# A gated S4D and spectral mix on one core: inputs of the states first, ScalarE in the parameters, the first rows from SBUF to SBUF, and one set of magnitudes at the start

## The chip, the cores and the metric

The kernel runs on one core of one Trainium2 chip. The metric is the device time of one execution in microseconds (us), and the median of several runs is compared. Engines are called by the names of the profile: PE is TensorE (PEld its weight loads), ACT is ScalarE, DVE is VectorE, POOL is GpSimd, SP is SyncE, which only issues DMAs here. ACT and POOL issue DMAs too; such issues stand in the profile as ACTq, POOLq and SPq.

## The reference

```python
def reference(A_u, A_log_A_real, A_A_imag, A_C_real, A_C_imag, A_log_dt, A_D_skip, B_x, B_w_r, B_w_i, gate_w):
    # A: u (1, 2048, 640), states N = 128 for each of the 640 channels
    dt = jnp.exp(log_dt)
    A = -jnp.exp(log_A_real) + 1j * A_imag
    C = (C_real + 1j * C_imag) * dt[:, None]
    P = jnp.exp((A * dt[:, None])[:, :, None] * pos[None, None, :])      # 640 x 128 x 2048
    K = 2.0 * jnp.einsum("dn,dnl->dl", C, P).real                        # the response, 640 x 2048
    y = irfft(rfft(u_t, 4096) * rfft(K, 4096))[:, :, :2048]              # long convolution
    a = y.transpose + u * D_skip
    # B: spectral filter of the same u
    b = irfft2(rfft2(u) * (w_r + 1j * w_i))
    g = sigmoid((u * gate_w).sum(-1))
    return g * a + (1 - g) * b
```

All data are f32.

## The kernel before, in words

The Fourier transforms of length 4096 are done as products with tables in two steps. Step 1 (`stage1`, line 335) takes four rows of four channels at a time, which are 16 matmuls in the profile; step 2 (`stage2`, line 348) goes by an index `pr` from 0 to 16, two at a time, each of which is 8 matmuls in the profile. The channels are four chunks `c` of 160, each in two halves `h` of 20 rows.

The program is made of five parts:

- **phase_p**, the parameters. The four inputs of the states (`cr`, `ci`, `ai`, `lar`, 128 x 5 x 128 each) and log_dt (`ld`) are loaded on SP. DVE computes the phase `ph` of C (with an Arctan on ACT) and the logarithm of its magnitude `q` (with an Ln on ACT); POOL computes the angle `th` and the decay `lar` of a step. `parts` splits each result into two f32r summands (a rounding copy, a subtraction) and writes them with a POOL DMA to `par_d` in device memory, where they are read again in another order.
- **phase_a, first half**: the transform of u, chunk by chunk: step 1 from `u`, with ACT evacuating PSUM into `t1` (line 382); the gate's logits (`p_g`, line 417) with weights `z` that POOL prepares (line 394); step 2 with `w2`, evacuated into `ut` and written to `u_d`. `copy` puts the evacuations on ACT until the marker `T.pin` is set and on DVE from then on. `T.pin` is the last matmul of step 2 for chunk 1 and the two indices from `pr` = 8.
- **phase_a, second half**: the spectral filter, nine fronts of 128 rows (lines 473 to 573).
- **phase_b**, the responses: 40 sets `t`, in batches of five (`BT`). `load` reads the `par` tile of a batch from `par_d`. `mags(t)` makes the magnitudes `e`: three matmuls (line 638) and three Exp (line 640). `phases(t)` makes the phases `q` (lines 649 to 652), `trig(t)` four Sin (lines 665 to 668), `prods(t)` the products `x` on DVE and `y` on POOL (lines 675 to 680), and `kgen(t)` 64 matmuls (line 693) into `p_k`. After every second set ACT copies `p_k` to `kt` (line 701); after ten sets `kt`, one tile of 40 rows, goes to `k_d` on SP (line 703).
- **phase_c and phase_d**: step 1 of the response's transform, then products with `u_d`, back transforms, gate and output.

Order: the instructions of an engine are issued in one fixed order, which is settled when the program is built: a scheduler goes by the order in which the code names them and by its own estimate of when they are ready. The code names first `ld` of phase_p (to its `yield`), then the loads of u and the first weights `z`, then the rest of phase_p, then phase_a as far as `T.pin`; from there `merge` interleaves phase_a and phase_c (`ga`, weight 194) with phase_b (`gl`, weight 76.8). `mags` puts each of its matmuls behind `T.pin` on PE, and the first Sin of a set behind the last Exp named before it, and an Exp behind the last Sin, so that ACT's function tables change only where a batch changes.

Of the kernel before, what the change touches and what calls it, by code (L numbers as in the profile page):

```python
# [9 lines left out]
F32 = mybir.dt.float32  # L10
F32R = mybir.dt.float32r
# [8 lines left out]
N = 128  # L20
# [163 lines left out]
def body(tc, A, out):  # L184
    nc = tc.nc
    T = Ctx()
    with ExitStack() as top:
# [7 lines left out]
        c1 = cst.tile([128, A["t_c1"].shape[1]], F32, name="c1")  # L195
        for x in (slice(0, 256), slice(256, c1.shape[1])):
            nc.scalar.dma_start(c1[:, x], A["t_c1"][:, x])
        o = 0
# [33 lines left out]
def phase_p(tc, A, T):  # L232
# [3 lines left out]
    with ExitStack() as ctx:  # L236
# [10 lines left out]
        yield 0.0  # L247
        lar, ai, cr, ci = tn("lar"), tn("ai"), tn("cr"), tn("ci")
        for t, nm in ((cr, "cr_l"), (ci, "ci_l"), (ai, "ai_l"), (lar, "la_l")):
            nc.sync.dma_start(t[:, :, :], A[nm])  # L250
# [19 lines left out]
        def parts(v, i, eng):  # L270
            t = p1.tile([128, 2, 5, N], F32R, name="parts%d" % i)
            eng.tensor_copy(t[:, 0], v[:, :, :])
            eng.tensor_tensor(out=t[:, 1], in0=v[:, :, :], in1=t[:, 0].bitcast(F32), op=ALU.subtract)
            G.dma_start(T.par_d[:, :, i:i + 2].rearrange("y x i z n -> (y x) (i z n)"), t.rearrange("p i z n -> p (i z n)").bitcast(F32))
# [3 lines left out]
        for o, i in ((ar, cr), (ab, ci)):  # L278
            V.tensor_scalar(out=o[:, :, :].bitcast(I32), in0=i[:, :, :].bitcast(I32), scalar1=0x7FFFFFFF, scalar2=None, op0=ALU.bitwise_and)
# [8 lines left out]
        V.tensor_scalar(out=ph[:, :, :], in0=ph[:, :, :], scalar1=1.0 / (2 * math.pi), scalar2=None, op0=ALU.mult)  # L288
        V.tensor_scalar(out=y[:, :, :], in0=ph[:, :, :], scalar1=-2.0, scalar2=0.25, op0=ALU.mult, op1=ALU.add)
        V.tensor_tensor(out=y[:, :, :], in0=y[:, :, :], in1=ab[:, :, :], op=ALU.mult)  # L290
        V.tensor_tensor(out=ph[:, :, :], in0=ph[:, :, :], in1=y[:, :, :], op=ALU.add)
        V.tensor_scalar(out=y[:, :, :], in0=ph[:, :, :], scalar1=-2.0, scalar2=0.5, op0=ALU.mult, op1=ALU.add)
        V.scalar_tensor_tensor(out=y[:, :, :], in0=cr[:, :, :], scalar=0.0, in1=y[:, :, :], op0=ALU.is_lt, op1=ALU.mult)
        V.tensor_tensor(out=ph[:, :, :], in0=ph[:, :, :], in1=y[:, :, :], op=ALU.add)
        V.tensor_scalar(out=y[:, :, :], in0=ci[:, :, :], scalar1=0.0, scalar2=-2.0, op0=ALU.is_lt, op1=ALU.mult)
# [57 lines left out]
def phase_a(tc, A, T):  # L353
# [3 lines left out]
    with ExitStack() as ctx:  # L357
# [44 lines left out]
        for c in range(4):  # L402
            t1 = ta[c % 2].tile([128, 16, 160, 2], F32, tag="t1", name="t1")
            t1v = t1.rearrange("p x d y -> p d x y")
            for h in range(2):
# [15 lines left out]
                if c < 3:  # L421
                    zs.append(weights(c + 1, h))
# [554 lines left out]
```

## Time and profile before

| | |
|---|---|
| time, median of 3 runs | 618.22 us (616.89 to 624.77) |
| the profiled execution's own time | 616.28 us |
| its span in the profile | 614.5 us, so 1.8 us lie around it |
| busy share of the span | PE 88%, PEld 67%, DVE 81%, ACT 59%, POOL 43% |
| DMA | 101.98 MB, mean 166 GB/s |

Busy shares are means over stages with different limits. The span has three stretches: the start, up to the first matmul of a response at 54.19 us; the middle, where `ga` and `gl` run beside each other, up to the first step 2 of phase_d at 437.84 us; and phase_d up to the end. The change touches the first and, through the order of the streams, the middle. The views that show waits name the engine and line that a wait ended on.

### The profile page before, as it was taken

To read this page: it belongs to the slowest core of one execution; us is meant where nothing else is said; L and a number is where in the kernel's file an instruction comes from. 1 tells how busy PE (TensorE), PEld (TensorE's weight loads), DVE (VectorE), ACT (ScalarE), POOL (GpSimd) and SP (SyncE) were. 2 spreads that over 40 slices of the span, in tenths; PEclk is the share of its full clock that TensorE was granted. 3 is DMA by queue.
4 is the path that set the end of the run, shared out by engine and by line. 5 is a ranking of instruction groups with operands and counts; after the bars stand their busy time and mean duration, and the time that the engine had idled before them with its cause. 6 is when DMAs were issued, how large, how long until landed. Compare 5 with 4: busy or idle time off the path is not lost.

```text
span 614.5 us, 16646 instructions
## 1 busy us (share of the span) xinstructions
PE 539.0 (88%) x7084; PEld 411.1 (67%) x7084; DVE 500.0 (81%) x748; ACT 364.6 (59%) x659; POOL 267.2 (43%) x246
## 2 busy tenths in 40 slices
PE   9688989989968989989799989898989979998864
PEld 6576667766746666766667766566878768787731
DVE  6961697598899988999999999978496975987863
ACT  4556675677847777897599897798523213231210
POOL 4921261152527344455326334345243546565450
PEclk9899989989979987999799999999989989999987
DMA  8787204154512411243242122115967989799985
GB/s 340 304 290 248 70 25 167 30 200 153 215 44 65 138 44 54 66 137 109 65 139 69 36 87 89 49 45 183 349 228 264 259 264 325 230 298 288 260 217 195
DMA packets 47987, 101.98 MB, mean 166 GB/s; under 512 B 3220, under 2 KB 32680, under 8 KB 46152
## 3 DMA queue, kind: packets, MB, share of 16 engines
q1 hardware_dynamic: 24792, 67.74, 34.0%
q10 hardware_dynamic: 20080, 22.52, 11.8%
q0 software_dynamic: 3040, 10.65, 5.3%
q8 instruction: 56, 0.92, 0.6%
q14 instruction: 19, 0.16, 0.1%
HBM read 60.91 MB, written 39.98 MB: 164 GB/s over the span
## 4 chain that ended last, share of the span: by engine, by line
PE 49%; DVE 26%; DMA 9%; ACT 9%; issue 4%; POOL 1%; ACTq 0%; SPq 0%; DVEq 0%; POOLq 0%
PE p_eo L551 8%; PE p_s L335 7%; PE p_s L348 7%; PE p_e L638 5%; PE p_k L693 4%; DMA s_d<-s 3%; PE p_i L814 3%; DVE q L652 2%; PE p_c L892 2%; PE p_p L649 2%; PE p_d L518 2%; PE p_i L565 2%; PE p_t L502 2%; DVE ma L795 2%; PE p_d L519 2%
## 5 line engine op out<-in xcount | busy, mean ns | idle before, releaser
L679 POOL TENSOR_TENSOR y<-e,sc 128x512 f32<-128x512 f32 x40 | 56.7, 1417 | 131.3 <-ACT sc L665 71.9
L348 PE MATMUL p_s<-t,w 128*64 128x160 f32 x1056 | 94.4, 317 | 10.3 <-ACT ut L382 4.5
L348 PEld LDWEIGHTS p_s<-t,w 128*64 128x64 f32 x1056 | 78.0, 140 | 21.2 <-ACT ut L382 5.4
L640 ACT ACTIVATE e<-p_e 128x512 f32<-128x512 f32 x120 | 68.6, 601 | 22.8 <-PE p_e L638 20.4
L551 PE MATMUL p_eo<-td,pmt 107*128 107x321 f32 x204 | 69.0, 458 | 3.9 <-ACT pmt L505 3.9
L693 PE MATMUL p_k<-x,y 128*32 128x64 f32 x2560 | 63.7, 229 | 9.9 <-DVE x L677 2.9
L693 PEld LDWEIGHTS p_k<-x,y 128*32 128x32 f32 x2560 | 46.1, 113 | 38.2 <-issue 29.4
L336 ACT COPY t<-p_s 128x512 f32<-128x512 f32 x40 | 24.5, 621 | 74.0 <-PE p_s L335 54.1
L652 DVE SCALAR_TENSOR_TENSOR q<-q,p_p 128x512 f32<-128x512 f32 x80 | 53.4, 681 | 13.5 <-ACT q L651 11.7
L638 PE MATMUL p_e<-rm,par 128*128 128x512 f32 x120 | 58.8, 520 | 3.4 <-ACT e L640 2.8
L680 POOL TENSOR_TENSOR y<-e,sc 128x512 f32<-128x512 f32 x40 | 54.4, 1359 | 6.5 <-ACT sc L666 6.5
L800 POOL TENSOR_TENSOR t<-ma 64x320 f32<-64x320 f32 x32 | 28.3, 883 | 60.5 <-DVE ma L795 50.8
L551 PEld LDWEIGHTS p_eo<-td,pmt 107*128 107x128 f32 x204 | 38.4, 198 | 19.5 <-ACT pmt L505 6.9
L677 DVE TENSOR_TENSOR x<-e,cx 128x1024 f32<-128x1024 f32 x40 | 48.5, 1213 | 2.2 <-ACT cx L668 2.2
L651 ACT ACTIVATE q<-p_p 128x512 f32<-128x512 f32 x80 | 46.5, 592 | 4.3 <-PE p_p L649 3.8
L335 PEld LDWEIGHTS p_s<-c,kt 128*64 128x64 f32 x640 | 41.2, 141 | 11.5 <-issue 6.7
L335 PE MATMUL p_s<-c,kt 128*64 128x128 f32 x640 | 45.2, 281 | 3.9 <-DVE mb L796 2.0
L814 PE MATMUL p_i<-t,w 128*64 128x160 f32 x528 | 45.0, 305 | 3.6 <-POOL t L801 2.8
L649 PE MATMUL p_p<-rp,par 128*128 128x512 f32 x80 | 43.3, 547 | 4.5 <-DVE q L652 4.4
L795 DVE TENSOR_TENSOR ma<-p_s,us 128x640 f32<-128x640 f32 (+1 forms) x36 | 28.2, 783 | 19.9 <-PE p_s L348 12.5
L814 PEld LDWEIGHTS p_i<-t,w 128*64 128x64 f32 x528 | 38.8, 139 | 8.0 <-POOL t L801 3.4
L816 ACT COPY s<-p_i 128x640 f32<-128x640 f32 x32 | 21.8, 693 | 37.6 <-PE p_i L814 28.5
(153 smaller groups left out, 1190.6 us busy)
## 6 DMA issues: line engine op xcount, KB each, us to landing
u_d<-ut SPq DMA_DIRECT2D x32, 320.0 KB, 2.7
us<-u_d ACTq DMA_DIRECT2D x16, 640.0 KB, 6.4
s_d<-s ACTq DMA_DIRECT2D x15, 640.0 KB, 8.6
t<-s_d SPq DMA_DIRECT2D x6, 1280.0 KB, 10.0
ww<-in_w_l SPq DMA_DIRECT2D x8, 642.0 KB, 4.0
ue<-u_d SPq DMA_DIRECT2D x8, 640.0 KB, 4.4
k_d<-kt SPq DMA_DIRECT2D x4, 1280.0 KB, 7.7
kt<-k_d SPq DMA_DIRECT2D x8, 640.0 KB, 9.2
```

The lines of the kernel that those rows point to most:

```text
L335: nc.tensor.matmul(p[64 * ri:64 * ri + 64, j, :], src(i + j), e1[ri], start=True, stop=True)
L348: ins = nc.tensor.matmul(p[64 * j:64 * j + 64, i, 160 * ri:160 * ri + 160], w2[:, x, 64 * ri:64 * ri + 64], t1[:, x // 2 if x < 32 else K0 ...
L551: P.matmul(p[:, :E], st.pmt[:DC, c, w, j, :], tv[:DC, w, c, :], start=c == 0, stop=c == 2)
L638: P.matmul(p[:, :], pars[t], rm[:, c:c + 512], start=True, stop=True)
L640: st.exp = S.activation(ef[:, c:c + 512], p[:, :], AF.Exp)
L649: P.matmul(p[:, :], pars[t], rp[:, c:c + 512], start=True, stop=True)
L652: V.scalar_tensor_tensor(out=qf[:, c:c + 512], in0=qf[:, c:c + 512], scalar=MAGIC, in1=p[:, :], op0=ALU.subtract, op1=ALU.subtract)
L677: V.tensor_tensor(out=x[:, 0].rearrange("p d (h j) -> p d h j", h=2), in0=e[:, :, 0:64].rearrange("p d (h j) -> p d h j", h=2), in1=cx.uns ...
L679: G.tensor_tensor(out=y[:, 1], in0=e[:, :, 64:96], in1=sc[:, 0], op=ALU.mult)
L680: G.tensor_tensor(out=y[:, 0], in0=e[:, :, 64:96], in1=sc[:, 1], op=ALU.mult)
L693: P.matmul(st.pb[32 * r:32 * r + 32, o, :], y[:, ri, 4 * qq + JR[r], :], x[:, ri, 4 * qq + JR[r], :], start=t % 2 + qq + 1 - ri == 0, stop ...
L814: T.mm = P.matmul(p[x:x + 64, i // 2, 160 * (i % 2):160 * (i % 2) + 160], T.w3[:, k0 + h + i, x:x + 64], t2[:, h + i, :], start=True, stop ...
```

## The change: what it does

- The loads of `cr` and `ci` are named ahead of those of u; `ai` and `lar` stay behind them. The gate weights `gw` are loaded between the two pieces of `c1` on ACT's queue, and all four `z` of chunks 0 and 1 are made at the start.
- In phase_p ACT takes the two absolute values, two squares and the four rounding copies of `parts`; two further DVE instructions go into neighbours as constants.
- `parts` also copies the rows of the first batch straight into a tile `par0` (two POOL DMAs of 16 partitions for each result, eight in all), which the first `load` then uses.
- `T.pin` is set at `pr` = 0 of chunk 1 instead of `pr` = 8.
- The magnitudes of set 0 are named alone; those of sets 1 to 4 follow behind the phases and the sines of set 0. From set 5 on the batches are as before.
- `kt` is a tile of eight rows in two buffers, written to `k_d` after every second set: twenty DMAs of 256 KB instead of four of 1280 KB.

```diff
+        T.gw = cst.tile([128, 4, 40], F32, name="gw")
         for x in (slice(0, 256), slice(256, c1.shape[1])):
             nc.scalar.dma_start(c1[:, x], A["t_c1"][:, x])
+            if x.start == 0:
+                nc.scalar.dma_start(T.gw[:, :, :], A["gw_l"])
...
+                    T.par0 = T.bc.tile([128, 5, N], F32R, name="par0")
...
         nc.sync.dma_start(ld[:, :], A["ld_l"])
-        yield 0.0
         lar, ai, cr, ci = tn("lar"), tn("ai"), tn("cr"), tn("ci")
         for t, nm in ((cr, "cr_l"), (ci, "ci_l"), (ai, "ai_l"), (lar, "la_l")):
+            if t is ai:
+                yield 0.0
             nc.sync.dma_start(t[:, :, :], A[nm])
...
             t = p1.tile([128, 2, 5, N], F32R, name="parts%d" % i)
-            eng.tensor_copy(t[:, 0], v[:, :, :])
+            S.copy(t[:, 0], v[:, :, :])
             eng.tensor_tensor(out=t[:, 1], in0=v[:, :, :], in1=t[:, 0].bitcast(F32), op=ALU.subtract)
+            for x in range(2):
+                G.dma_start(T.par0[i + x::8], t[0:16, x])
             G.dma_start(T.par_d[:, :, i:i + 2].rearrange("y x i z n -> (y x) (i z n)"), t.rearrange("p i z n -> p (i z n)").bitcast(F32))
...
         for o, i in ((ar, cr), (ab, ci)):
-            V.tensor_scalar(out=o[:, :, :].bitcast(I32), in0=i[:, :, :].bitcast(I32), scalar1=0x7FFFFFFF, scalar2=None, op0=ALU.bitwise_and)
-        V.tensor_tensor(out=mx[:, :, :], in0=ar[:, :, :], in1=ab[:, :, :], op=ALU.max)
+            S.activation(o[:, :, :], i[:, :, :], AF.Abs)
+        V.scalar_tensor_tensor(out=mx[:, :, :], in0=ar[:, :, :], scalar=1.2e-38, in1=ab[:, :, :], op0=ALU.max, op1=ALU.max)
         V.tensor_tensor(out=q[:, :, :], in0=ar[:, :, :], in1=ab[:, :, :], op=ALU.min)
-        V.tensor_scalar(out=mx[:, :, :], in0=mx[:, :, :], scalar1=1.2e-38, scalar2=None, op0=ALU.max)
...
-        V.tensor_scalar(out=ph[:, :, :], in0=ph[:, :, :], scalar1=1.0 / (2 * math.pi), scalar2=None, op0=ALU.mult)
...
-        V.tensor_tensor(out=w[:, :, :], in0=ff, in1=ff, op=ALU.mult)
-        V.tensor_tensor(out=q[:, :, :], in0=q[:, :, :], in1=q[:, :, :], op=ALU.mult)
+        S.activation(w[:, :, :], ff, AF.Square)
+        S.activation(q[:, :, :], q[:, :, :], AF.Square)
...
-        ap = pool("a_p", 2)
+        ap = pool("a_p", 4)
...
-        zs = [weights(0, 0), weights(0, 1)]
+        zs = [weights(c, h) for c in (0, 1) for h in (0, 1)]
...
-                if (c, pr) == (1, 8):
+                if (c, pr) == (1, 0):
                     T.pin = ins
...
-        par = w2.tile([128, BT, N], F32R, tag="par", name="par")
-        G.dma_start(par[:, :, :], par_v[b0 // BT])
+        if b0 == 0:
+            par = T.par0
+        else:
+            par = w2.tile([128, BT, N], F32R, tag="par", name="par")
+            G.dma_start(par[:, :, :], par_v[b0 // BT])
...
-            S.copy(kt[:, i:i + 8, :], st.pb[:, :, :])
-            if t % 10 == 9:
-                nc.sync.dma_start(T.k_d[c], kt[:, :, :])
+            kt = w2.tile([128, 8, 64], F32, tag="k", name="kt")
+            S.copy(kt[:, :, :], st.pb[:, :, :])
+            nc.sync.dma_start(T.k_d[c, :, i:i + 8], kt[:, :, :])
...
-            if t % BT == 0:
+            batch = t == 1 or t % BT == 0
+            if batch:
                 if t:
                     prods(t - 1, rs[t - 1])
                     pend.append(t - 1)
-                for x in range(t, t + BT):
+                for x in range(t, 1 if t == 0 else t - t % BT + BT):
                     yield from mags(x)
...
-                if t + BT < 40:
+                if t % BT == 0 and t + BT < 40:
                     load(t + BT)
...
-            if t % BT:
+            if not batch:
                 prods(t - 1, rs[t - 1])
                 pend.append(t - 1)
```

More of the change, by code (lines that the diff above doesn't have):

```diff
@@ L368, in phase_a @@
         ps = ctx.enter_context(tc.tile_pool(name="a_ps", side="right", reuse_waits="tile", bufs=3, space=PSUM))
-        gw = ac.tile([128, 4, 40], F32, name="gw")
+        gw = T.gw
         lg = ac.tile([128, 8, 64], F32, name="lg")
@@ L396, in weights @@
             return z
-        nc.scalar.dma_start(gw[:, :, :], A["gw_l"])
         load(0, 0)
         load(0, 1)
-        zs = [weights(0, 0), weights(0, 1)]
+        zs = [weights(c, h) for c in (0, 1) for h in (0, 1)]
         for c in range(4):
@@ L420, in phase_a @@
                 S.copy(lg[:, 2 * c + h, :], p[:, :])
-                if c < 3:
-                    zs.append(weights(c + 1, h))
+                if c < 2:
+                    zs.append(weights(c + 2, h))
             for pr in range(0, 17, 2) if c < 3 else (8, 10, 12, 14, 16, 0, 2, 4, 6):
@@ L683, in kgen @@
         x, y = xy.pop(t)
-        if t % 10 == 0:
-            st.kt = w1.tile([128, 40, 64], F32, tag="k", name="kt")
-        kt = st.kt
         if t % 2 == 0:
```

8 lines of the change are left out of this document (4 added, 4 removed).

## The prediction

> **What bounds the kernel now.** I read the busy shares first, then a table of stretches around the start, then the timeline of those stretches.
>
> ```profile
> span 614.5 us, 16646 instructions
> PE 539.0 (88%) x7084; PEld 411.1 (67%) x7084; DVE 500.0 (81%) x748; ACT 364.6 (59%) x659; POOL 267.2 (43%) x246
> ```
>
> No engine is full over the span, but two are near it, so the next view is the busy time in stretches. The columns are the stretch, its length, and the busy time of PE, PEld, DVE, ACT and POOL.
>
> ```profile
> 8.90:41.40 32.50, 24.52 (x439) 22.37 (x436) 31.83 (x29) 19.03 (x37) 22.41 (x18) 0.95 0.84 329
> 41.40:54.00 12.60, 11.84 (x212) 11.12 (x208) 0.00 (x0) 7.47 (x16) 4.25 (x5) 1.00 0.89 265
> 54.00:69.60 15.60, 14.52 (x136) 9.43 (x132) 6.11 (x11) 10.08 (x17) 0.00 (x0) 1.00 0.35 132
> 69.60:92.00 22.40, 19.03 (x401) 14.16 (x399) 20.32 (x32) 16.56 (x29) 14.10 (x11) 0.92 0.17 47
> 92.00:120.00 28.00, 27.32 (x395) 20.72 (x390) 18.53 (x34) 15.72 (x26) 2.74 (x3) 1.00 0.30 108
> 150.00:430.00 280.00, 251.09 (x3008) 183.10 (x3007) 257.88 (x382) 223.08 (x416) 123.22 (x105) 0.95 0.29 91
> 420.00:437.90 17.90, 15.45 (x379) 13.00 (x369) 8.93 (x14) 14.19 (x27) 5.81 (x5) 1.00 0.63 224
> ```
>
> Up to 41.4 us DVE is full with the parameters. From 41.4 to 54 us it does nothing, and from 54 to 69.6 us little (6.11 of 15.6): the magnitudes are made, and DVE has no phases yet. But PE, with the transform of u, is idle for only 0.76 of 12.6 us and 1.08 of 15.6 us there. From 69.6 to 92 us DVE is full (20.32 of 22.4) and PE waits 3.37 us; from 92 to 120 us PE is full again (27.32 of 28). The two take turns. So the hole in DVE, 12.6 + 9.5 = 22.1 us, looks like the prize, but PE could win only 0.76 + 1.08 + 3.37 = 5.2 us from 41.4 to 92 us, plus part of the 8.0 us that it misses before 41.4 us.
>
> What released the responses:
>
> ```profile
> 2.59 0.43 SPq L250 DMA_DIRECT2D cr<-in_cr_l  x1
> 8.99 0.74 DVE L279 TENSOR_SCALAR ar<-cr 128x640 int32<-128x640 int32 x1 [3.38 <-DMA cr<-in_cr_l]
> 40.49 0.83 DVE L273 TENSOR_TENSOR parts<-q,parts 128x640 fp32r<-128x640 f32 x1
> 41.62 0.53 POOL L274 DMA_DIRECT2D par_d<-parts  x1 [2.39 <-DVE parts L273]
> 46.27 6.46 PE L348 MATMUL p_s<-t,w 128*64 128x160 f32 x88
> 47.94 1.14 POOL L628 DMA_DIRECT2D par<-par_d  x2 [4.50 <-DMA par_d<-parts]
> 54.19 0.73 PE L638 MATMUL p_e<-rm,par 128*128 128x512 f32 x2
> 54.76 1.28 ACT L640 ACT_TABLE_LOAD   x1 [1.03 <-issue]
> par<-par_d POOLq DMA_DIRECT2D x8, 320.0 KB, 3.9
> w<-in_t_w SPq DMA_DIRECT2D x1, 64.0 KB, 1.9
> ```
>
> Two gates closed within two microseconds of each other. The parameters were on chip at about 47.94 + 0.57 + 3.9 = 52.4 us (one of the two issues, then the landing). The marker was 80 matmuls behind 46.27 us at 73 ns (6.46 / 88), 52.1 us, and later by a stall of PE. The first response matmul is at 54.19 us. Opening either gate alone would gain 1.8 to 2.1 us; the change opens both.
>
> **The change part by part.** Rows for it, from the groups of the first 42 us (DVE), 75 us (ACT) and 60 us (POOL), busy us and mean ns of one behind the bar:
>
> ```profile
> L291 DVE TENSOR_TENSOR ph<-ph,y 128x640 f32<-128x640 f32 x1 | 3.6, 3587 | 0.0
> L294 DVE TENSOR_TENSOR ph<-ph,y 128x640 f32<-128x640 f32 x1 | 0.8, 826 | 0.0
> L288 DVE TENSOR_SCALAR ph<-ph 128x640 f32<-128x640 f32 x1 | 0.5, 487 | 0.0
> L283 DVE RECIPROCAL w<-mx 128x640 f32<-128x640 f32 x1 | 4.1, 4140 | 0.0
> L287 ACT ACTIVATE ph<-q 128x640 f32<-128x640 f32 x1 | 0.7, 736 | 3.5 <-DVE q L284 3.5
> L394 POOL TENSOR_TENSOR z<-c,gw 128x640 f32<-128x640 f32 x6 | 7.6, 1278 | 6.5 <-DMA gw<-in_gw_l 6.5
> L274 POOL DMA_DIRECT2D par_d<-parts x4 | 2.3, 570 | 8.7 <-DVE parts L273 8.7
> ```
>
> *Parameters on DVE.* L291 and L294 are the same operation at 3.59 and 0.83 us; the long one ran while POOL worked. At the short prices the chain is 12 one-input operations of 0.49, 16 of 0.83 and the reciprocal of 4.14: 23.3 us, where 31.8 us were measured, so 8.5 us are the price of POOL beside it. The change removes six of the first kind and two of the second, 4.6 us. `cr` and `ci` go ahead of three loads of u; L279 waited for `cr` until 8.99 us, 6.4 us after its issue. Issued about 1.4 us earlier and with nothing large ahead, they land between 2 and 6.4 us after it; I take 4, which starts the chain 3.6 us sooner. Against it stand new hand-overs between DVE and ACT, 0 to 4 us; I take 2. The last part is then ready at 41.3 - 4.6 - 3.6 + 2 = 35.1 us, 32 to 38 by these ends.
>
> *Rows straight to `par0`.* The write of `par_d` (41.62 to 47.94 us) and its reading back (to 52.4 us), 6.3 and 4.5 us, go from this path; two issues of 0.57 and a landing of 1.9 (64 KB) to 3.9 us (320 KB) take their place. Near 40 KB each, I take 2: parameters at 38 us, 35 to 43, and hidden behind the marker in any case. On POOL eight issues of 0.57 cost 4.6 us more and two roundings go; two `z` of 1.28 us move ahead of `th`, which delays POOL's half by 2.6 us. That half ended before DVE's, so it costs nothing until DVE is that much faster.
>
> *The marker.* 16 matmuls behind 46.27 us is 47.4 us, so the responses' gate moves from 54.2 to 47.4 us if phase_a keeps its pace. It hardly does: eight operations of 0.74 us, 5.9 us, are added on ACT, which is busy 19.03 of 32.5 us there, so the sum fits. But ACT takes its work in order:
>
> ```profile
> 17.57 1.91 PE L348 MATMUL p_s<-t,w 128*64 128x160 f32 x24 [1.70 <-DMA w<-in_t_w]
> 20.90 0.74 ACT L287 ACTIVATE ph<-q 128x640 f32<-128x640 f32 x1 [3.46 <-DVE q L284]
> 22.01 5.22 PE L348 MATMUL p_s<-t,w 128*64 128x160 f32 x48 [2.53 <-ACT ut L382]
> 37.02 0.42 ACT L382 COPY ut<-p_s 64x320 f32<-64x320 f32 x1 [3.88 <-DMA u_d<-ut]
> ```
>
> When the Arctan waited 3.46 us for DVE, the evacuations queued behind it and PE lost 2.53 us. The change makes eight more places of this kind. The delay of phase_a lies between -2.5 us (DVE earlier, the Arctan no longer late, the wait for `u_d` at 37 us absorbed) and 4.2 us (rival B); I take 1.0, nearest to the added work that does not fit under a wait. The first load of u comes later by two issues, about 1 us; that lies under PE's wait of 1.70 us for `w2` and costs as much if that load came sooner. The Trainium skill's page "Perfetto Trace Analysis" (section Per-engine timelines) says the queues of ACT, DVE and GpSimd are strictly first in, first out; these rows agree.
>
> *One set of magnitudes first.* Set 0's work on DVE moves ahead of the other four magnitudes:
>
> ```profile
> L652 DVE SCALAR_TENSOR_TENSOR q<-q,p_p 128x512 f32<-128x512 f32 x80 | 53.4, 681 | 13.5 <-ACT q L651 11.7
> L677 DVE TENSOR_TENSOR x<-e,cx 128x1024 f32<-128x1024 f32 x40 | 48.5, 1213 | 2.2 <-ACT cx L668 2.2
> 70.19 0.60 ACT L651 ACTIVATE q<-p_p 128x512 f32<-128x512 f32 x1 [0.60 <-PE p_p L649]
> 70.81 1.28 ACT L667 ACT_TABLE_LOAD   x1
> 72.11 0.60 ACT L667 ACTIVATE sx<-q 128x512 f32<-128x512 f32 x1
> ...
> 71.61 0.69 DVE L662 TENSOR_SCALAR aq<-q 128x1024 int32<-128x1024 int32 x1
> L675 DVE SCALAR_TENSOR_TENSOR x<-e,sx x40: 669/680/697, 74.0 to 427.5; 128x512 f32<-128x512 f32 x40
> L676 DVE TENSOR_TENSOR x<-e,sx x40: 672/681/692, 74.6 to 428.1; 128x512 f32<-128x512 f32 x40
> ```
>
> Five operations of 0.68 or 0.69 (L652 twice) and one of 1.21 are 4.6 us on DVE, out of the full stretch from 69.6 us into the empty one. The price is two more table changes, 1.28 us each: behind L651's end at 70.79 us the next activation starts at 72.11 us, so 1.3 us a switch and 2.6 us in all, under ACT's 5.5 idle us from 54 to 69.6; uncovered it costs those 2.6 us. The page "ScalarE: Activation LUTs" of the Trainium skill (What ACT_TABLE_LOAD costs; Table sets) speaks against this step: do all calls of one set first, since a switch is 1.28 us plus a drain of 1.38. By it two switches would be 5.3 us, and the forecast 2.7 us later at worst; the row shows no drain of that size.
>
> *What this wins.* PE's work up to 92 us is the same, so the win is PE's idle time. Of 5.2 us I take 4.0; the ends are 0 (DVE's idle time was no limit) and 5.2. *The tail of the middle:* `ga` has eight more indices of 0.55 yields behind the marker, 4.4 units on top of 194 under unchanged weights, so `gl` ends 4.4 units earlier, about one set, inside the first transform of K. There PE misses 2.45 us (420 to 437.9). I take 0.5, from -1 to 2.4. DVE's evacuations of chunk 1 (eight, which take ACT 0.42 us each in the row of line 382 above) fall into its empty time.
>
> *`kt` in eight rows.* Same copies, same bytes. SP gets 16 more issues, each behind a copy of ACT:
>
> ```profile
> SPq L703 <- ACT kt L701: 20.6, 4, 6.9
> SPq L478 <- DVE mm L537: 53.7, 7, 16.1
> ```
>
> SP waits long for its buffers anyway (the second row), so I take nothing, up to rival D's price.
>
> Sum: -4.0 + 1.0 - 0.5 = -3.5 us on the profiled execution's 616.3 us, 612.8 us. The median of the runs shown (618.2) stands 1.9 us above that execution; I add 1.0 us for a median of its kind: **613.8 us**.
>
> **The rivals.**
>
> A, nothing moves: PE is the bound from 41 to 69 us and again from 92 us, so an earlier marker only reorders its work, and phase_a's delay eats the rest. For it: 11.84 of 12.6 us. Against: 3.37 us lost behind DVE. -1 + 1 on 616.3 and 1.0 for the median: 617.3 us.
>
> B, slower: ACT blocks. DVE and POOL run 8.5 us behind their undisturbed pace, ACT so far paid 3.5 us of it, since the last roundings were not its own; now they are, and phase_a loses up to 8.5 - 3.5 = 5.0 us before the marker, less the 0.8 us of PE's idle time that it absorbs. It decides from the point where a rounding waits over 1 us for DVE or POOL. 616.3 + 4.2 + 1.0: 621.5 us. For it: 2.53 us of PE lost this way already.
>
> C, DVE is the true bound of the middle (257.88 of 280 us, against 251.09 for PE): then both the 6.8 us of the marker and the 4.6 us of set 0 come through. 616.3 - 11.4 + 1.0: 605.9 us. Against: `gl` also ends earlier, and DVE is idle at the end for longer.
>
> D, SP's order: twenty issues waiting 5.15 us each (20.6 / 4) are 103 us of SP's time, and loads of the filter stand behind them. If each of its nine fronts came 1.5 us late, 13.5 us are lost: 630.8 us. Against: L478 shows that the loads wait for buffers rather than for SP.
>
> **How the numbers follow.** Forecast 0.42 (610 to 616), A 0.22, B 0.16, C 0.15, D 0.05. The range from 605 to 622 leaves out D and the far halves of B and C. About 2% (12.4 us) is what a measurement of this kernel can tell from no change: under 605.8 us lies a little over half of C, over 630.6 us half of D and a rest for an order I have not foreseen. Faster 0.09, same 0.86, slower 0.05.
>
> **What would show it.** Parameters: the last part near 35 us and the first response matmul at 48 to 49 us. ACT: no wait of a rounding over 2 us. Set 0: its phases on DVE at about 52 us, one more load of the Exp table and one of the Sin table. PE idle from 42 to 85 us down to 1 or 2 us. End: phase_d's first step 2 at 434 us instead of 437.84. I am wrong if that start moves by over 8 us or not at all, if ACT waits for POOL's `th`, or if SP's waits at `k_d` grow beyond 100 us with loads of the filter late behind them.

## The result, and the profile after

| | before | after |
|---|---|---|
| time, median | 617.67 us (616.13 to 624.77, 6 runs) | 636.03 us (634.71 to 637.63, 6 runs) |
| ratio | | 1.028 (95% interval 1.0229 to 1.0331) |
| profiled execution | 616.28 us, span 614.5 | 634.71 us, span 632.9 |

The changed kernel is slower by 2.8%. The forecast was 613.8 us, within 605 to 622. Ratios and their intervals, here and below, leave disturbed executions out (seven of the ten of e10), which medians and ranges do not, and a stretch of a disturbed profile is not compared (its places in the table below are empty), but for the start of g2. First the busy shares of the changed kernel:

```profile
span 632.9 us, 16705 instructions
PE 549.4 (87%) x7084; PEld 412.4 (65%) x7084; DVE 495.9 (78%) x748; ACT 369.5 (58%) x661; POOL 261.9 (41%) x251
```

The same 7084 matmuls keep PE busy for 10.4 us longer than before (539.0 us). Next the two kernels in four stretches: up to the first matmul of a response, up to the last one, up to the first product `ma` of phase_d, and phase_d. The columns are the stretch, its length, busy time of PE, PEld, DVE, ACT and POOL, the granted clock, the share of DMA, GB/s. Before:

```profile
0.00:54.20 54.20, 44.01 (x713) 38.26 (x713) 34.95 (x47) 29.63 (x57) 28.85 (x28) 0.97 0.85 306
54.20:402.10 347.90, 314.40 (x4025) 229.42 (x4023) 307.13 (x468) 262.30 (x477) 139.82 (x116) 0.95 0.29 95
402.10:439.20 37.10, 33.37 (x642) 25.49 (x643) 23.29 (x34) 31.52 (x60) 14.98 (x13) 1.00 0.50 168
439.20:614.50 175.30, 147.25 (x1712) 117.97 (x1708) 134.62 (x199) 41.12 (x66) 83.56 (x89) 0.95 0.87 263
```

And after:

```profile
0.00:60.10 60.10, 43.33 (x649) 36.98 (x649) 32.02 (x40) 31.57 (x57) 32.83 (x36) 0.83 0.75 263
60.10:415.40 355.30, 322.12 (x4079) 231.33 (x4078) 302.40 (x470) 264.18 (x478) 129.88 (x113) 0.95 0.30 97
415.40:456.30 40.90, 36.00 (x653) 27.02 (x653) 26.70 (x41) 32.66 (x61) 15.54 (x13) 1.00 0.48 155
456.30:632.90 176.60, 147.97 (x1712) 117.10 (x1708) 134.80 (x199) 41.08 (x66) 83.61 (x89) 0.94 0.85 258
```

The 18.4 us of the span are 5.9 in the start, 7.4 between the first and the last response, 3.8 behind it and 1.3 in phase_d. So two places have to be explained: the start, and the middle with its tail, 11.2 us together. The first response is not at the same place of PE's work, though: since the marker moved, 649 matmuls lie ahead of it instead of 713, and 64 of step 2 are 4.7 us at 73 ns (6.46 us for 88). For equal work the start lost 10.6 us, and the middle with its tail 6.5.

The marks of the two gates, from the timeline of the changed kernel (start, duration, engine, line):

```profile
36.60 0.83 DVE L278 TENSOR_TENSOR parts<-q,parts 128x640 fp32r<-128x640 f32 x1 [0.79 <-ACT parts L277]
36.86 0.49 POOL L280 DMA_DIRECT2D par<-parts  x1 [0.46 <-ACT parts L277]
60.07 0.72 PE L645 MATMUL p_e<-rm,par 128*128 128x512 f32 x2
```

The parameters come at 37.4 us, 4 us sooner than before, and go straight to `par0`. But the first response waits for the marker until 60.07 us, where 54.19 us was the mark of before. PE's first 47 us, the start of the changed kernel:

```profile
1.44 3.38 PE L383 MATMUL p_w<-lg 128*128 128x512 f32 x4 [1.44 <-DVE lg L379]
7.66 6.25 PE L340 MATMUL p_s<-c,u 128*64 128x128 f32 x80 [2.83 <-DMA u<-in_u_l]
13.84 0.77 PE L421 MATMUL p_g<-u,z 128*32 128x64 f32 x40
14.53 4.59 PE L340 MATMUL p_s<-c,u 128*64 128x128 f32 x80
27.60 1.29 PE L421 MATMUL p_g<-u,z 128*32 128x64 f32 x40 [8.48 <-ACT t L387]
28.83 2.40 PE L353 MATMUL p_s<-t,w 128*64 128x160 f32 x16
33.81 2.46 PE L353 MATMUL p_s<-t,w 128*64 128x160 f32 x24 [2.58 <-ACT lg L424]
36.95 9.32 PE L353 MATMUL p_s<-t,w 128*64 128x160 f32 x92 [0.68 <-ACT ut L387]
```

PE waits 2.83 us for u, then 8.48 us for three evacuations. What stood ahead of these on ACT, and the DVE operation that ACT waited for:

```profile
16.55 0.64 ACT L387 COPY t<-p_s 128x512 f32<-128x512 f32 x1 [0.25 <-PE p_s L340]
17.20 1.28 ACT L293 ACT_TABLE_LOAD   x1
18.50 0.74 ACT L293 ACTIVATE ph<-q 128x640 f32<-128x640 f32 x1
21.60 0.74 ACT L308 ACTIVATE w<-fr 128x640 f32<-128x640 f32 x1 [2.37 <-DVE fr L306]
...
24.20 0.72 ACT L277 CAST parts<-lar 128x640 fp32r<-128x640 f32 x1 [0.61 <-POOL lar L329]
24.94 1.28 ACT L311 ACT_TABLE_LOAD   x1
26.23 0.74 ACT L311 ACTIVATE q<-q 128x640 f32<-128x640 f32 x1
26.88 1.61 ACT L387 COPY t<-p_s 128x512 f32<-128x512 f32 x3
32.91 0.73 ACT L277 CAST parts<-ph 128x640 fp32r<-128x640 f32 x1 [4.42 <-DVE ph L301]
...
17.41 4.16 DVE L306 TENSOR_SCALAR fr<-mx 128x640 int32<-128x640 int32 x1
```

Between 17.2 and 26.9 us ACT does nothing but parameters: in the one order that was settled for it, three evacuations of step 1 stand behind the Arctan, the squares, two roundings and the Ln. One of these waited 2.37 us for a DVE operation that took 4.16 us beside POOL. In the kernel before, all ten evacuations of chunk 0's step 1 stand ahead of the Arctan and its table; the last one there:

```profile
15.22 0.63 ACT L382 COPY t<-p_s 128x512 f32<-128x512 f32 x1 [0.25 <-PE p_s L335]
15.93 0.21 ACT L420 COPY lg<-p_g 128x64 f32<-128x64 f32 x1
16.16 1.28 ACT L287 ACT_TABLE_LOAD   x1
```

### The profile page after: what moved, and what is told of

Read it like the earlier page. It is cut to its first block, busy times and chain, and to the rows that moved or that the text cites. A ratio compares the mean times of both kernels' runs of the same rounds, so it can differ in the third digit from the quotient of the medians.

```text
span 632.9 us, 16705 instructions
## 1 busy us (share of the span) xinstructions
PE 549.4 (87%) x7084; PEld 412.4 (65%) x7084; DVE 495.9 (78%) x748; ACT 369.5 (58%) x661; POOL 261.9 (41%) x251
## 4 chain that ended last, share of the span: by engine, by line
PE 46%; DVE 29%; ACT 11%; DMA 7%; issue 4%; ACTq 1%; POOL 0%; SPq 0%; DVEq 0%; POOLq 0%
PE p_s L340 7%; PE p_s L353 7%; PE p_e L645 6%; PE p_eo L555 5%; DVE q L659 3%; DMA s_d<-s 3%; PE p_k L697 3%; PE p_i L819 3%; PE p_i L569 3%; DVE x L684 3%; PE p_c L897 3%; DVE aq L669 2%; PE p_t L506 2%; DVE ma L800 2%; PE p_d L522 2%
## 5 line engine op out<-in xcount | busy, mean ns | idle before, releaser
L686 POOL TENSOR_TENSOR y<-e,sc 128x512 f32<-128x512 f32 x40 | 53.7, 1343 | 150.3 <-ACT sc L672 100.7
L353 PE MATMUL p_s<-t,w 128*64 128x160 f32 x1056 | 99.3, 323 | 8.1 <-ACT lg L424 2.6
L645 PE MATMUL p_e<-rm,par 128*128 128x512 f32 x120 | 62.3, 532 | 7.4 <-ACT e L647 5.9
L555 PE MATMUL p_eo<-td,pmt 107*128 107x321 f32 x204 | 64.8, 441 | 0.0
L687 POOL TENSOR_TENSOR y<-e,sc 128x512 f32<-128x512 f32 x40 | 55.5, 1387 | 5.4 <-ACT sc L673 5.3
L387 DVE COPY ut<-p_s 128x320 f32<-128x320 f32 (+1 forms) x49 | 22.9, 486 | 40.8 <-PE p_s L353 39.9
L340 PE MATMUL p_s<-c,u 128*64 128x128 f32 x640 | 45.2, 284 | 3.8 <-DMA u<-in_u_l 2.8
L555 PEld LDWEIGHTS p_eo<-td,pmt 107*128 107x128 f32 x204 | 37.1, 190 | 13.6 <-ACT pmt L509 1.2
L656 PE MATMUL p_p<-rp,par 128*128 128x512 f32 x80 | 42.0, 529 | 3.5 <-DVE q L659 3.4
```

The lines of the kernel that those rows point to most:

```text
L340: nc.tensor.matmul(p[64 * ri:64 * ri + 64, j, :], src(i + j), e1[ri], start=True, stop=True)
L353: ins = nc.tensor.matmul(p[64 * j:64 * j + 64, i, 160 * ri:160 * ri + 160], w2[:, x, 64 * ri:64 * ri + 64], t1[:, x // 2 if x < 32 else K0 ...
L555: P.matmul(p[:, :E], st.pmt[:DC, c, w, j, :], tv[:DC, w, c, :], start=c == 0, stop=c == 2)
L645: P.matmul(p[:, :], pars[t], rm[:, c:c + 512], start=True, stop=True)
L686: G.tensor_tensor(out=y[:, 1], in0=e[:, :, 64:96], in1=sc[:, 0], op=ALU.mult)
L687: G.tensor_tensor(out=y[:, 0], in0=e[:, :, 64:96], in1=sc[:, 1], op=ALU.mult)
```

## Experiments

Ratios are of a kernel's time to that of the kernel before on the same chip, with the 95% interval. The columns of us split the span of the profiled execution at the first `p_e` and at the first `ma`, as above.

| kernel | ratio | to the first response | from there to phase_d | phase_d |
|---|---|---|---|---|
| before | | 54.2 | 385.0 | 175.3 |
| after | 1.028 (1.0229 to 1.0331) | 60.1 | 396.2 | 176.6 |
| e1_act_back | 1.0195 (1.0124 to 1.0266) | 53.9 | 399.3 | 173.5 |
| e2_act_alone | 1.0028 (0.9987 to 1.0069) | 58.9 | 381.3 | 176.7 |
| e7_round_back | 1.009 (1.0043 to 1.0136) | | | |
| e6_kd_pool | 1.0316 (1.0216 to 1.0417) | 60.3 | 392.9 | 174.7 |
| e5_pin_back | 1.0227 (1.0145 to 1.0308) | 64.5 | 383.4 | 176.9 |
| e11_pin_mags_back | 1.0188 (1.0119 to 1.0257) | 64.8 | 384.2 | 175.1 |
| e13_pin_alone | 1.0116 (1.0067 to 1.0165) | 52.1 | 394.8 | 173.8 |
| e12_mags_alone | 1.0000 (0.9956 to 1.0043) | 57.1 | 383.8 | 173.1 |
| f1_loads_z_back | 1.0221 (1.0126 to 1.0316) | 55.2 | 392.1 | 175.0 |
| f2_loads_z_kt | 1.0108 (1.003 to 1.0187) | 61.5 | 387.2 | 174.9 |
| f3_start_back | 1.002 (0.997 to 1.007) | 54.7 | 383.5 | 176.5 |
| e10_kt_alone | 0.9964 (0.9899 to 1.0029) | | | |
| g1_fill | 1.0266 (1.0189 to 1.0343) | | | |
| g2_marker_kept | 1.0151 (1.0063 to 1.0239) | 49.7 | | |
| g3_start_back_fill | 1.0113 (1.0073 to 1.0152) | 59.6 | 385.8 | 172.8 |
| g4_fill9 | 1.0279 (1.021 to 1.0348) | 61.7 | 396.0 | 175.7 |
| g5_pin_weight | 0.9846 (0.979 to 0.9902) | 51.2 | 376.4 | 174.9 |
| g6_pin_late | 1.0043 (1.0008 to 1.0078) | 60.1 | 383.3 | 175.6 |

One reading of the table carries the rest. The fourth column falls in two groups: 381.3 to 387.2 us with the marker at `pr` = 8 or 14, and 392.1 to 399.3 us with the marker at `pr` = 0 and the weight 194 left as it was. Only g5, with the marker at 0 and another weight, stands apart, at 376.4. Of the gap between the groups, 4.7 us are the 64 matmuls that the marker moves behind the first response.

The third column comes from one profile of each kernel, and it scatters. The kernel before, e12, e13 and g5 have the same matmuls in the same order up to step 2 of chunk 1, and that begins at 46.27, 48.14, 48.12 and 48.81 us. The first response of e12, whose marker is that of before, is 2.9 us later.

### ScalarE's share

e1 is the changed kernel with all of this edit, e7 the changed kernel with its first two lines (the four roundings), and e2 the kernel before with its reverse alone.

```diff
-            S.copy(t[:, 0], v[:, :, :])
+            eng.tensor_copy(t[:, 0], v[:, :, :])
...
-            S.activation(o[:, :, :], i[:, :, :], AF.Abs)
+            V.tensor_scalar(out=o[:, :, :].bitcast(I32), in0=i[:, :, :].bitcast(I32), scalar1=0x7FFFFFFF, scalar2=None, op0=ALU.bitwise_and)
...
-        S.activation(w[:, :, :], ff, AF.Square)
-        S.activation(q[:, :, :], q[:, :, :], AF.Square)
+        V.tensor_tensor(out=w[:, :, :], in0=ff, in1=ff, op=ALU.mult)
+        V.tensor_tensor(out=q[:, :, :], in0=q[:, :, :], in1=q[:, :, :], op=ALU.mult)
```

> The changed kernel with the eight ACT operations of the parameters (two absolute values, two squares, four rounding copies) back on DVE and POOL; all else as changed. Theory S (the start): ACT, in order, held the evacuations of the transform of u behind its share of the parameters, so that PE lost 6.6 us more idle time and some 8.5 us of clock before the first response matmul. Then this kernel has PE's wait of 8.5 us before the first gate matmuls gone, the first response matmul at 50 to 54 us, and takes 622 to 627 us. Theory M (the middle: SP's queue with twenty writes of k_d, or the new order of the magnitudes): 630 to 636 us, the start earlier and the middle longer.

> The kernel before with only those eight operations moved to ACT (loads, marker, magnitudes, kt and par0 as before). Theory S: PE waits several us between 17 and 37 us, the granted clock there falls below 0.8, and the time is 625 to 631 us. Theory M: 615 to 620 us, as before.

> The changed kernel with only the four rounding copies back on DVE and POOL; absolute values and squares stay on ACT. Theory S in the form of rival B (the roundings that wait for DVE and POOL are what blocks): as good as the kernel with all eight back, 622 to 627 us. Theory S by mere volume (any ACT work between the evacuations costs): half way, 628 to 632 us. Theory M: 632 to 637 us.

Measured: 628.18 us (627.4 to 629.09) for e1, 618.59 (613.39 to 621.08) for e2, 623.88 (617.13 to 783.91) for e7. Of theory S, e7 is in the range that rival B's form gave; e1 (622 to 627) and e2 (625 to 631) are not. The roundings weigh most: taking them alone from ACT (e7) gives back two thirds of the loss, clear of noise. Taking all eight operations away (e1) gives back a third, and its interval overlaps that of the changed kernel: DVE has the squares again there, the Ln on ACT waits 6.66 us for DVE, and PE 7.37 us behind it. The share alone costs the kernel before nothing that can be told. Its start looks slower; from the timeline of e2:

```profile
18.28 1.36 PE L348 MATMUL p_s<-t,w 128*64 128x160 f32 x16
27.48 4.01 PE L348 MATMUL p_s<-t,w 128*64 128x160 f32 x32 [7.84 <-ACT lg L420]
```

PE waits 7.84 us, and the first response comes at 58.9 us, 4.7 us later than before and 1.8 later than in e12. But the stretch behind is shorter than before by 3.7 us, so that phase_d begins only 0.9 us later. Why it is shorter stays open.

### SP's queue

e6 is the changed kernel with the writes of `k_d` issued by POOL:

```diff
-            nc.sync.dma_start(T.k_d[c, :, i:i + 8], kt[:, :, :])
+            G.dma_start(T.k_d[c, :, i:i + 8], kt[:, :, :])
```

> The changed kernel with the twenty writes of kt issued by POOL instead of SP. Theory S: SP's wait at them (143 us) hides behind nothing that is late, 634 to 638 us. Theory M with SP's queue as the cause: 622 to 629 us, and the loads and writes of the filter issued earlier.

e10 is the kernel before with kt in eight rows:

```diff
...
-                nc.sync.dma_start(T.k_d[c], kt[:, :, :])
+            kt = w2.tile([128, 8, 64], F32, tag="k", name="kt")
...
+            nc.sync.dma_start(T.k_d[c, :, i:i + 8], kt[:, :, :])
```

> The kernel before with kt in eight rows alone. L and R: 616 to 619 us, no difference from before, as the prediction took it. If SP's longer waits at the writes of k_d delay loads of the filter (rival D of the prediction): 622 us or more, with the first step 2 of phase_d late by as much.

In the changed kernel SP waited long at these writes (queue and line, waited for, us in total, times, longest):

```profile
SPq L707 <- ACT kt L706: 143.4, 14, 19.6
```

With the writes on POOL (e6) the time is 634.31 us (629.72 to 638.38) and its interval overlaps that of the changed kernel. kt alone (e10) gives 0.9964 (0.9899 to 1.0029), but by three executions; the median of all ten is 622.29 us (610.0 to 627.14). f3 below has kt in eight rows too and stands at 1.002. In the changed kernel the loads of the filter are issued later (the last of `ww` at 401.6 instead of 369.9 us), yet DVE waits 0.5 us for `ww` in all. So no cost of SP's long waits can be told.

### Marker and magnitudes

e5 is the changed kernel with the marker's line of this edit, e11 with both parts; e13 is the kernel before with the reverse of the first part alone, e12 with the reverse of the second alone (set 0's magnitudes first).

```diff
-                if (c, pr) == (1, 0):
+                if (c, pr) == (1, 8):
...
-            batch = t == 1 or t % BT == 0
+            batch = t % BT == 0
...
-                for x in range(t, 1 if t == 0 else t - t % BT + BT):
+                for x in range(t, t + BT):
```

> The changed kernel with the marker back at pr = 8 of chunk 1; all else as changed. PE's order behind the first 368 matmuls is then nearly that of the kernel before (3655 of 3752 in the same order). Theory P (the earlier marker shifts the two interleaved streams against each other, and the new order of the middle is worse by 11 to 14 us): the stretch from the first response matmul to phase_d falls from 396 to about 384 us and the time to 618 to 624 us. Theory Q (the magnitudes of set 0 alone, with their extra table changes, or kt, lengthen the middle): 630 to 636 us.

> The changed kernel with the marker and the magnitudes both as before; loads, ACT's share, par0 and kt as changed. PE's order is then that of the kernel before (3749 of 3752). Theory P: within 2 us of the kernel with the marker alone put back, 618 to 624 us. Theory Q: clearly faster than that kernel, by 5 us or more, which stands at 630 or above.

> The kernel before with the marker alone moved to pr = 0; PE still waits there for the parameters by way of device memory. Theory P: the middle is longer by 11 us or more and the time is 627 to 634 us. Theory Q: 615 to 621 us.

> The kernel before with the magnitudes of set 0 alone ahead of its phases and those of sets 1 to 4 behind; nothing else. Theory P: 614 to 620 us, two table loads more on ACT without effect, or a gain of up to 4 us from DVE's earlier start. Theory Q: 624 us or more.

Measured: e5 631.75 us, e11 628.55, e13 622.09 (620.31 to 630.5), e12 615.88 (612.25 to 621.39). The times of e5 and e11 miss the 618 to 624 us of theory P, and that of e13 lies between the ranges of the two theories; e12 is where P put it. The magnitudes change nothing that can be told, alone (1.0000) or taken back (e5 and e11 overlap). The marker alone costs 1.2%, although it brings the first response forward by 2.1 us: the stretch to phase_d becomes 9.8 us longer, 4.7 us of it by the 64 matmuls that moved. Phase_d begins 7.7 us later than before. Up to there PE is idle for 46.8 us instead of 47.4, but busy for 400.1 instead of 391.8 us: the loss is not idle time, it is the same work at a lower granted clock (0.94 instead of 0.96). In e5 the marker's going back has two sides: the first response falls to 64.5 us, and the stretch behind it is again that of before. So the changed kernel has both losses: its start is about 10 us late (64.5 against 54.2), of which the early marker takes 4.4 back, and the marker then costs 12.8 in the stretch behind (396.2 against 383.4), 8.4 us in sum. In time this pair is less clear: the intervals of e5 and of the changed kernel overlap.

### Loads and z

f2 is the kernel before with this edit and, for space, kt in eight rows; f1 is the changed kernel with its reverse; f3 is the changed kernel with ScalarE's share, the loads, z and the marker all as before.

```diff
         nc.sync.dma_start(ld[:, :], A["ld_l"])
-        yield 0.0
...
+            if t is ai:
+                yield 0.0
...
-        zs = [weights(0, 0), weights(0, 1)]
+        zs = [weights(c, h) for c in (0, 1) for h in (0, 1)]
```

> The changed kernel with the loads of u again ahead of those of cr and ci and with two z at the start as before; ScalarE's share of the parameters, the marker, par0, the small kt and the one set of magnitudes stay. Theory L (the late first load of u, and z of chunk 1 ahead of the transform, start the loss of the first 40 us): step 1 begins near 5.1 us again, the first response matmul near 54 us (it was 60.1 us), and some 6 us of the 18.4 us come back: 627 to 631 us. Theory R (the hand-overs between DVE and ScalarE do it whatever the order of the loads): first response matmul still after 58 us, 633 to 638 us.

> The kernel before with the changed order of the loads, four z at the start, and kt in eight rows (without the small kt the four z do not fit the memory); parameters on DVE and POOL, marker and magnitudes as before. Theory L: PE loses 3 to 6 us in the first 40 us, 620 to 624 us. Theory R: the start keeps the pace of before, since ScalarE has nothing of the parameters to wait for, 616 to 619 us.

> The changed kernel with ScalarE's share, the order of loads and of z, and the marker all as before; only the direct way to par0, the constants of the arctangent, the small kt and the one set of magnitudes stay. If the start and the marker are the whole cause (L and R agree here): 615 to 619 us. If something that stays costs time by itself, par0's eight issues or kt in eight rows: 622 us or more.

Measured: f1 627.63 us (624.1 to 632.82), f2 622.55 (619.25 to 625.42), f3 616.86 (612.07 to 623.7). Each is in the range that theory L gave. In f1 the first response comes at 55.2 us, near the 54 of theory L; its time alone would not rule out theory R, since its interval reaches 1.0316. In f2, without any of ScalarE's share, the start already goes wrong; PE in its timeline:

```profile
7.57 6.25 PE L336 MATMUL p_s<-c,u 128*64 128x128 f32 x80 [2.34 <-DMA u<-in_u_l]
13.75 0.77 PE L418 MATMUL p_g<-u,z 128*32 128x64 f32 x40
14.45 4.59 PE L336 MATMUL p_s<-c,u 128*64 128x128 f32 x80
24.36 1.29 PE L418 MATMUL p_g<-u,z 128*32 128x64 f32 x40 [5.32 <-ACT t L383]
```

Step 1 begins 2.4 us later than before, and again three of its evacuations stand behind the Arctan, which waits for DVE:

```profile
22.99 0.74 ACT L288 ACTIVATE ph<-q 128x640 f32<-128x640 f32 x1 [4.61 <-DVE q L285]
23.63 1.60 ACT L383 COPY t<-p_s 128x512 f32<-128x512 f32 x3
```

That is 5.32 us of PE, and the first response comes 7.3 us later than before (4.4 later than in e12). Loads and z were not tried apart. Both may have a part: `q`, for which the Arctan waits, starts on DVE at 21.09 us where it was 19.54 before, although `cr` and `ci` came sooner, and POOL works on four z from 7.28 to 13.54 us.

At the first response the two parts add up. It is at 49.7 us in g2 below, which has neither, at 53.9 in e1 (loads and z), at 55.2 in f1 (ScalarE's share) and at 60.1 in the changed kernel (both). f3 shows that the rest of the change (`par0`, the constants, kt, the magnitudes) is worth nothing that can be told.

### The clock of the start, and the marker by itself

g1 is the changed kernel with this edit, which adds throwaway matmuls into PE's waits; g4 has nine instead of four of them ahead of `p_g`. g3 is f3 with two such matmuls behind `pr` = 0 of chunk 0. g2 is f3 with the marker at (1, 0).

```diff
-        for _ in range(2):
+        for _ in range(3):
             P.matmul(p[:, :], z[:, 0:128], z, start=True, stop=True)
...
+                if (c, h) == (0, 1):
+                    for _ in range(4):
+                        P.matmul(T.fill[:, :], T.id, T.c1[:, 0:512], start=True, stop=True)
                 p = ps.tile([128, 64], F32, tag="ps", name="p_g")
```

> The changed kernel with throwaway matmuls in two of PE's waits of the start, into a bank that nothing reads: one more of 128x512 among those of line 383 (fills most of the 2.83 us before the first step 1), and four of 128x512 ahead of the gate sums of chunk 0's second half (about 6.8 of the 8.48 us in which PE waits for ScalarE). The rest of the order on PE is the same. Theory K (the clock that a wait costs is a loss of its own): the granted clock stays at 1.0 from 8 to 11 us and from 21 to 31 us, the first 80 matmuls of step 1 take 4.7 us instead of 6.25, and of the 4.7 us that the low clock cost in the first 60 us, 2 to 4 come through: 632 to 634 us. Theory W (PE waits for ScalarE in any case, the clock only goes along): the clock rises as well but the first response matmul stays at 60 us, 635 to 638 us.

> The changed kernel with ScalarE's share and the orders of loads and z as before; the marker, par0, kt and the one set of magnitudes stay. Against f3_start_back this differs in the marker alone. If the marker costs by itself as it did in the kernel before (7.2 us by the ratio 1.0116): 622 to 626 us, with the first ma of phase_d near 446 us though the first response matmul is near 52 us. If the marker costs only together with the late start: 615 to 618 us.

> f3_start_back with two throwaway matmuls of 128x512 behind the first row of step 2 of chunk 0, where PE waits 4.48 us for ScalarE at 18.6 us and the clock is halved from 19.4 to 25.5 us. Theory K: the clock stays at 1.0 there, the next 56 matmuls take about 4.1 us instead of 5.56, and up to 1.5 us come through: 614 to 617 us, at best a little under the kernel before. Theory W: 616 to 618 us, no difference from f3_start_back or from before.

> g1_fill with nine instead of four throwaway matmuls ahead of the gate sums of chunk 0's second half: 8.3 us at the 0.93 us that one took there (3.70 us for four), in a wait of 9.8 us. Theory K (the clock is a loss of its own): granted clock 1.0 from 8 to 31 us, the 40 matmuls of the gate sums 0.77 us instead of 1.42, the first 24 of step 2 about 1.9 us instead of 3.47, the first response matmul at 57 to 58 us, 2 to 4 us less than the changed kernel. Theory W (ScalarE paces PE there, the clock only goes along): the same rows shorten, but the first response matmul stays at 59 to 60 us and the time within 2 us of the changed kernel's 1.028 times the time before.

In the changed kernel PE's granted clock falls behind its waits. The stretches from 20 to 30 and from 30 to 40 us, after, then the same of g4:

```profile
20.00:30.00 10.00, 2.40 (x50) 2.11 (x52) 9.86 (x8) 6.25 (x9) 9.82 (x10) 0.57 0.35 118
30.00:40.00 10.00, 6.74 (x58) 5.15 (x56) 6.43 (x8) 4.05 (x10) 5.54 (x11) 0.67 0.80 266
```

```profile
20.00:30.00 10.00, 7.61 (x69) 3.74 (x67) 9.86 (x8) 6.24 (x9) 9.82 (x10) 1.00 0.40 126
30.00:40.00 10.00, 4.28 (x32) 3.34 (x34) 6.54 (x8) 3.40 (x8) 5.54 (x11) 0.66 0.71 232
```

g4's throwaway matmuls do what they should: the clock is 1.00 up to 30 us. And it wins nothing: 633.46 us (630.73 to 635.2), 1.0279, the first response at 61.7 us, later than either theory said. The next wait, for ACT, comes at the same place and the clock falls there instead. So theory W holds for this wait: ScalarE sets PE's pace, and the clock goes along. g1, where the matmuls ran for only 3.7 us, took 631.18 us (625.23 to 634.87), below both ranges, and decides nothing. g3 does not test the two theories: its two matmuls were placed elsewhere, at 9.1 and 18.0 us, one of them in the middle of step 1. With these 2.25 us more work on PE ahead of step 2 (1.12 and 1.13 us) the first response came 4.9 us later than in f3 and the ratio is 1.0113 instead of 1.002.

g2 has the start of before and the early marker. From its tile `p_e` (number, shortest, median and longest ns, first and last start):

```profile
L644 PE MATMUL p_e<-rm,par x120: 388/502/989, 49.7 to 409.5; 128*128 128x512 f32 x120
```

The first response is at 49.7 us, 4.5 us earlier than before, and the kernel is slower by 1.5% (1.0063 to 1.0239); its 624.93 us (616.56 to 627.03) are in the range forecast for a marker that costs by itself, as it did in e13.

### The weight of the merge

g5 is the kernel before with this edit:

```diff
-                if (c, pr) == (1, 8):
+                if (c, pr) == (1, 0):
...
-            merge((194.0, ga), (76.8, gl))
+            merge((198.4, ga), (76.8, gl))
```

g6 is the kernel before with the marker moved the other way:

```diff
-                if (c, pr) == (1, 8):
+                if (c, pr) == (1, 14):
```

> The kernel before with the marker at (1, 0) and the weight of the first stream raised from 194 to 198.4, the 4.4 units that now stand behind the marker. Theory H (the marker costs because the two streams run at another rate against each other, the responses ending a set early): 615 to 618 us, the cost of the marker alone (ratio 1.0116) gone. Theory O (any order but the tuned one costs, or responses before chunk 1's step 2 cost by themselves): 620 to 625 us.

> The kernel before with the marker at (1, 14), three pairs of rows later, so responses begin about 4 us later. Theory E (early responses cost, so late ones gain): 611 to 615 us. Theory O (the order before is a good one among others): 618 to 625 us. Theory G (the gate of the responses was worth what the prediction said, 1.8 to 4 us): 619 to 622 us, with the first ma of phase_d later by 2 to 4 us.

g5 takes 606.7 us (604.32 to 615.47), ratio 0.9846 (0.979 to 0.9902): faster than the kernel before by 1.0 to 2.1%, and below the ranges of both theories. g6 takes 618.48 us (614.23 to 621.23), 1.0043, and its phase_d starts 4.2 us later. Early responses are no loss by themselves (theory E falls); at the early marker, the weight decides. That is what theory H said, though it did not foresee that the pair gains. It is not shown that the weight has to follow the marker: 198.4 with the marker at `pr` = 8 was not run, nor in the changed kernel, and may be the better number there too. The second and third stretch of e13, then of g5:

```profile
52.10:405.90 353.80, 323.25 (x4076) 235.08 (x4077) 301.63 (x468) 261.35 (x476) 128.26 (x116) 0.94 0.30 96
405.90:446.90 41.00, 36.05 (x655) 27.08 (x655) 26.76 (x42) 32.67 (x61) 15.50 (x13) 1.00 0.44 139
```

```profile
51.20:391.70 340.50, 313.56 (x4088) 227.27 (x4087) 306.37 (x476) 261.43 (x477) 133.37 (x116) 0.98 0.31 101
391.70:427.60 35.90, 32.96 (x645) 25.05 (x645) 23.21 (x35) 31.39 (x60) 14.92 (x13) 1.00 0.54 185
```

The two differ in one number of the merge. Behind the last response 5.1 us go, which fits streams that end together again. In the stretch ahead of it 13.3 us go: PE does the same matmuls in 9.7 us less at a clock of 0.98 instead of 0.94, and waits 3.6 us less. Why this order keeps the clock up and the other doesn't stays open.

## Why the prediction was wrong, point by point

- **Parameters**: right. The last part was ready at 37.4 us, in the 32 to 38 forecast, and `par0` closed no gate. (The ends that the prediction names for its terms, 1.4 to 5.8 us from the load and 0 to 4 of hand-overs, give 30.9 to 39.3 us and not 32 to 38.)
- **The delay of phase_a**, the step that failed first. It was sized at 1.0 us, with 4.2 us as its worst end. Without it the first response is at 49.7 us (g2); in the changed kernel it is at 60.07, so it was 10.4 us, in single profiles. Rival B named the mechanism, ACT's work in order with roundings that wait (one waited 4.42 us, and e7 shows that they weigh most), but priced it from the 3.5 us that ACT waited in the trace of before. It missed that the order is settled anew and a wait on ACT holds every evacuation that then stands behind it: PE lost 8.48 us at one place, 2.58 at the next.
- **The first load of u**, costed at nothing under PE's wait of 1.70 us for `w2`. It was issued 0.95 us later, as forecast (2.12 against 1.17 us), but step 1 began 2.5 us later (7.66 against 5.13 us) and took 6.25 instead of 4.76 us, since the clock was halved for part of it. That is 4.0 us, and the cover was 1.70. The loads and z, with kt but without ScalarE's share, cost 1.1% (f2).
- **The marker**: the two gates were read rightly, and g2 opens at 49.7 us where 48 to 49 was forecast for them. What they win was not: forecast -4.0 us of PE's idle time, set 0 included, measured +7.2 (1.16% of 616.62, e13). From 42 to 85 us PE is idle for 4.2 us in e13, 1.5 of them for `par`, where it was 3.6 before: little of the idle time that the term counted on was won, and the work got slower.
- **The tail of the middle**, taken as a gain of 0.5 us, between a loss of 1 and a gain of 2.4: this term had the wrong sign and left out the stretch ahead of it. The text itself noted that `ga` has 4.4 units more behind the marker under unchanged weights, and read that as the responses ending a set early, a gain. The tail grew by 3.8 us (3.9 in e13), and with the other weight the early marker gains 1.5% instead of losing 1.2%.
- **One set of magnitudes**: neither its price nor its gain can be told (e12, 1.0000). One more table load of each kind appears, as forecast:

```profile
L647 ACT ACT_TABLE_LOAD x9 | 11.5, 1283 | 1.3 <-PE p_e L645 1.2
L674 ACT ACT_TABLE_LOAD x9 | 11.5, 1283 | 0.2
```

  Nine where eight were, 1283 ns each. The interval of e12 is about 2.7 us wide to either side, so a price of 2.6 us lies just inside it. The 5.3 us that the prediction estimated from the Trainium skill ("ScalarE: Activation LUTs", What ACT_TABLE_LOAD costs) would lie outside, unless idle time of ACT hid it or DVE's earlier start made up for it.
- **kt and rival D**: nothing that can be told, as forecast. The first half of the mark named for D appeared (SP waits 143.4 us at `k_d`), and the loads of the filter were issued later, but DVE hardly waited for them (0.5 us for `ww`).
- **Rival C** gave 605.9 us, near g5's 606.7, but for another reason: DVE is busy 306.37 of 340.5 us in g5's middle, not full, and PE's time is what fell.

All terms counted PE's idle time and took its work as constant. Up to phase_d PE was idle 54.8 instead of 47.4 us, but it was also busy 401.5 instead of 391.8 us with the same 5376 matmuls.

## What to carry to other kernels

When a marker that starts one stream moves, the weights that share out the rest between the streams are worth trying again: here the same marker cost 1.2% with the old number and gained 1.5% with another. Work that goes to an engine with one fixed order is to be priced by the evacuations that stand behind its longest wait once the order is settled, not by the sum of its durations. And the time of the first response says little about the end: 58.9 us went with no loss (e2), 49.7 us with a loss of 1.5% (g2).

## What the runs showed of the hardware

The granted clock was halved behind some short waits of PE. The first 80 matmuls of step 1 took 6.25 us behind 2.83 us of waiting (after; clock 0.50 from 8 to 11 us) and behind 2.34 us (f2; 0.50 from 9 to 12 us). In the kernel before, the same matmuls with no wait, and 48 of them behind 2.52 us:

```profile
5.13 4.76 PE L335 MATMUL p_s<-c,u 128*64 128x128 f32 x80
...
37.49 2.84 PE L335 MATMUL p_s<-c,u 128*64 128x128 f32 x48 [2.52 <-ACT ut L382]
```

Both have 59 ns for one, so that wait did not halve the clock; the wait of 2.53 us at 22.01 us, quoted in the prediction, did: its 48 matmuls took 5.22 us, 109 ns for one, and 59 that followed at 28.47 us took 78 ns. In e12, with the same matmuls in the same order, it is the other way round:

```profile
22.16 3.62 PE L348 MATMUL p_s<-t,w 128*64 128x160 f32 x48 [2.94 <-ACT ut L382]
...
37.69 4.51 PE L335 MATMUL p_s<-c,u 128*64 128x128 f32 x48 [2.59 <-ACT ut L382]
```

From 23 to 25 us the clock is 0.50 before and 1.00 in e12; from 38 to 40 us it is 1.00 before and 0.50 in e12. So neither the length of such a wait nor its place in the program decides alone, and two executions of the same start can differ by this. The Trainium skill's page "TensorE: Matmul & The Clock Gate" (Part 1: The HAM clock gate) gives a free-running window of about 3.4 us that must be idle; that the outcome differs between executions agrees, the length doesn't, since 2.34 us was enough here. An integer operation of DVE on 128x640, 1.00 us for the same operation before and 0.49 at its shortest there, took 4.16 us while POOL worked (L306 above).
